# Moving a weight clamp from VectorE to GpSimd, and a subtraction of maxima from ScalarE to VectorE

## The chip, the core and the metric

One core of a Trainium2 chip runs the whole program. Its engines work side by side, each through its own queue in a fixed order: TensorE (PE, with its weight loads listed as PEld), VectorE (DVE), ScalarE (ACT), GpSimd (POOL) and SyncE (SP, which only issues transfers here). The metric is the device time of one execution in microseconds, the median of three runs.

## The reference

A linear attention with random-feature style exponentials feeds a two-layer mixer.

```python
# q, k, v: (8, 8, 576, 64) float32; w_phi: (64, 128) float32
proj = x @ w_phi                                    # for q and for k
proj = proj - max(abs(proj), axis=-1)
phi  = concat([exp(proj), exp(-proj)], axis=-1)     # 256 features
kv, z = k_phi^T @ v, sum_s(k_phi)
attn = (q_phi @ kv) / (q_phi @ z + 1e-6)            # -> x: (8, 576, 512)
u   = x + (relu(x^T @ w_tok1) @ w_tok2)^T           # token mix, 576 -> 256 -> 576
out = u + relu(u @ w_ch1) @ w_ch2                   # channel mix, 512 -> 1536 -> 512
```

The four mixer weights come as float64. The output is float32.

## The kernel before

**Precision.** Most products are made of reduced-width float32 (`F32R`) pieces: each operand is split into a high part and the remainder, and `mm3` (L77) adds three products. The splitting is `split` (L69): one engine casts, another subtracts.

**Five streams.** `keys` (L259) walks over the 32 head pairs: projection `ppk`, the row maximum `mx` of the absolute values (L226), `pm` = projection minus maximum (L228 to L234), two exponentials (L278) and the sums `pkv` (L300). `queries` (L317) does the same for the query side (`ppq`, and `ppt` for the left-over 64 rows), turns `pm` over on TensorE (`pt`, L356), takes exponentials (L363) and forms numerators and denominators (`pn`, L389 and `mm3`), a reciprocal (L401) and the product with it on GpSimd (L402). `token_mix` (L416) runs per batch and per half of the channels, `channel_mix` (L462) per 256 tokens: `h` (up), `acc` (down). `load_weights` (L144) fetches and converts the weights.

**The first four pairs are plain.** For pairs 0 to 3 (`PLAIN = 4`) the attention multiplies whole float32 operands (L216, L389 with 64-row or float32 operands) instead of split ones. `less_max` (L191) tells three cases apart by `base`: `base == D` are the plain keys, `base == 0` the plain queries and their left-over rows, `base is None` the split ones. In the plain cases `pr` is the PSUM bank itself. For plain keys VectorE subtracts the maximum from the bank (L234, `eng` is `nc.vector`). For plain queries VectorE negates the maximum (`nmx`, L230) and ScalarE adds it as a bias, one activation per 128 columns (L232). For the split pairs `pr` is an SBUF tile and GpSimd subtracts (L234).

**The conversion of the weights** is `convert` (L114), called 31 times: 7 times for `w1` and `w2` (tiles named `bits`), 24 times for `wc1` and `wc2` (tiles named `bitsc`, all 128 x 512). A float64 is read as two 32-bit words, `top` and `low`. ScalarE takes the absolute value of `top`, seen as a float32 (L131); VectorE clamps it to `LEAST`, `MOST` (L132), shifts it (L133), puts the sign in (L134) and the highest bits of `low` (L135); ScalarE casts the high part (L72) and GpSimd subtracts it (L75). The tile `m` is one of four buffers with the tag `g`, which `channel_mix` uses too.

**What sets the order.** `weave` (L547) lets the streams take turns by a virtual clock, and so makes the program's order. The scheduler of the language then lays the instructions on each engine's queue, by priority and by a simulated timeline that knows a duration for each instruction. So an edit of one instruction can move its neighbours on every engine. The order is fixed when the program is built; at run time each engine works its queue from front to back and waits on semaphores.

Of the kernel before, what the change touches and what calls it, by code (L numbers as in the profile page):

```python
# [8 lines left out]
F32 = mybir.dt.float32  # L9
# [8 lines left out]
P = 128  # L18
# [24 lines left out]
def mixer_kernel(ctx, tc, qk, vm, vt, w_phi, w1, w2, wc1, wc2d, out):  # L43
# [70 lines left out]
    def convert(hi, lo, srcs, name, tag=None):  # L114

        w, n = hi.shape
        if tag is None:
            tag = f"late{nstage[0] % STAGES}"
            nstage[0] += 1
        raw = wk.tile([P, 4, 256], U32, tag=tag, name=f"raw{name}", bufs=3 if tag == "xt1" else 1)  # L120
        raw = raw.rearrange("p a b -> p (a b)")[:w, :2 * n]
        at = 0
        for src in srcs:
            m = src.shape[1]
            nc.sync.dma_start(raw[:, 2 * at:2 * (at + m)].bitcast(I64), src)
            at += m
        raw = raw.rearrange("p (n two) -> p n two", two=2)
        top, low = raw[:, :, 1], raw[:, :, 0]
        m = streamed(wk, [P, 512], U32, tag="g", name=f"bits{name}", bufs=4)[:w, :n]

        nc.scalar.activation(m.bitcast(F32), top.bitcast(F32), AF.Abs)  # L131
        nc.vector.tensor_scalar(m.bitcast(F32), m.bitcast(F32), LEAST, MOST, op0=ALU.max, op1=ALU.min)  # L132
        nc.vector.tensor_scalar(m, m, 3, 0x3FFFFFF8, op0=ALU.logical_shift_left, op1=ALU.bitwise_and)  # L133
        nc.vector.scalar_tensor_tensor(m, top, 0xC0000000, m, op0=ALU.bitwise_and, op1=ALU.bitwise_or)  # L134
        nc.vector.scalar_tensor_tensor(m, low, 29, m, op0=ALU.logical_shift_right, op1=ALU.bitwise_or)  # L135
        split(hi, lo, m.bitcast(F32), nc.scalar, nc.gpsimd)
# [54 lines left out]
    def less_max(ts, units, name, base=None):  # L191
# [33 lines left out]
        mx = column(wk, 2, tag=f"mx{kind}", name=f"mx{name}")  # L225
        nc.vector.tensor_reduce(mx[:, :n], pr, axis=AX.X, op=ALU.max, apply_absolute_value=True)  # L226
        pm = wk.tile([P, 2, F], F32, tag=f"pm{kind}", name=f"pm{name}", bufs=1 if kind == "t" else 2)
        if base == 0:  # L228
            nmx = column(wk, 2, tag="nmx", name=f"nmx{name}")
            nc.vector.tensor_scalar(nmx[:, :n], mx[:, :n], -1.0, None, op0=ALU.mult)  # L230
            for i in range(n):
                nc.scalar.activation(pm[:, i], pr[:, i], AF.Identity, bias=nmx[:, i:i + 1])  # L232
        else:
            eng.tensor_tensor(pm[:, :n], pr, mx[:, :n].unsqueeze(2).to_broadcast([P, n, F]), op=ALU.subtract)  # L234
        return pm

    nplain = {"k": 0, "q": 0}
# [372 lines left out]
```

## Time and profile before

| | |
|---|---|
| median of three runs | 1180.97 us (1180.92 to 1181.36) |
| profiled execution, span from first to last instruction | 1183.6 us |
| TensorE busy | 1137.6 us (96%) |
| VectorE busy | 867.1 us (73%) |
| ScalarE busy | 531.5 us (45%) |
| GpSimd busy | 587.1 us (50%) |
| mean granted TensorE clock | 0.975 |

The profile holds one execution, a little longer than the runs' median: its span is 2.6 us above it. A time of the page for what lies around the span is not given. Busy shares are averages over the whole span; the program has stretches of different character, so the same numbers by stretch say more. "Idle before" is what an engine stood still ahead of a group, with the engine that released it. The granted clock is the share of TensorE's full speed in a stretch. Where two engines' rows overlap in time at an unusual length, one may be held up by the other without a semaphore.

### The profile page before, as it was taken

The numbers are of one execution on the slowest core, as the hardware profiler recorded it, in microseconds if no ns is written. First come the engines' busy times: TensorE is split into PE (matmuls) and PEld (weight loads), VectorE is DVE, ScalarE is ACT, GpSimd is POOL, SyncE is SP. The second block draws the span as 40 slices with busy tenths as digits, with TensorE's granted clock in tenths as the row PEclk, the third lists the DMA queues.
The fourth block names the chain that finished last, engine by engine and source line by source line (L and its number), as shares of the span: only waits on it lengthen the run. The fifth ranks groups of instructions, "written<-read, shape, count | busy, mean of one in ns | idle before, by whom it ended". The sixth has DMA issues, their size and how long they took to land.

```text
span 1183.6 us, 24087 instructions
## 1 busy us (share of the span) xinstructions
PE 1137.6 (96%) x9032; PEld 1102.0 (93%) x9032; DVE 867.1 (73%) x1782; ACT 531.5 (45%) x1545; POOL 587.1 (50%) x734
## 2 busy tenths in 40 slices
PE   8789897899999999999999999999999999999998
PEld 7667887898999999999999999999999999999998
DVE  7977899986777888887878677684787978763111
ACT  5767565453444445444444443343353544431110
POOL 3344775854555566465555455473564655431000
PEclk9679898999999999999999999999999999999999
DMA  9541222111111111111111011110111110000000
GB/s 232 150 135 28 72 84 71 50 31 28 31 40 32 49 31 32 49 32 49 32 34 46 20 31 49 30 50 1 49 31 49 32 48 12 19 1 19 19 19 19
DMA packets 65300, 54.31 MB, mean 46 GB/s; under 512 B 44768, under 2 KB 56416, under 8 KB 65184
## 3 DMA queue, kind: packets, MB, share of 16 engines
q1 hardware_dynamic: 63824, 52.41, 15.4%
q8 instruction: 72, 1.18, 0.4%
q10 hardware_dynamic: 1360, 0.36, 0.2%
q14 instruction: 44, 0.36, 0.1%
HBM read 43.32 MB, written 9.44 MB: 45 GB/s over the span
## 4 chain that ended last, share of the span: by engine, by line
PE 78%; DVE 11%; ACT 4%; issue 3%; POOL 2%; DMA 2%; SPq 0%; DVEq 0%; POOLq 0%; ACTq 0%
PE h L81 23%; PE acc L81 23%; PE pkv L300 8%; PE pn L81 7%; PE ph L81 3%; PE pa L81 3%; PE pt L356 3%; PE ppq L212 2%; PE ppk L212 2%; DVE qh L74 2%; PE pn L389 1%; DVE den L401 1%; PE px L423 1%; DMA rawc<-in_wc 1%; DVE bitsc L132 1%
## 5 line engine op out<-in xcount | busy, mean ns | idle before, releaser
L81 PE MATMUL acc<-gh,wc 128*128 128x256 f32 x1728 | 345.1, 283 | 0.0
L81 PEld LDWEIGHTS acc<-gh,wc 128*128 128x128 f32 x1728 | 276.0, 188 | 0.2 <-ACT gh L489 0.2
L81 PE MATMUL h<-uh,wc_h 128*128 128x256 f32 x864 | 246.8, 286 | 4.3 <-ACT wc_h L72 2.2
L81 PE MATMUL h<-uh,wc_l 128*128 128x256 f32 x864 | 245.9, 285 | 0.8 <-POOL wc_l L75 0.8
L81 PE MATMUL h<-ul,wc_h 128*128 128x256 f32 x864 | 243.9, 282 | 0.3 <-POOL ul L470 0.3
L81 PE MATMUL acc<-gl,wc 128*128 128x256 f32 x864 | 242.0, 282 | 0.6 <-DVE gl L490 0.6
L278 ACT ACTIVATE kp<-pmk 128x256 f32<-128x256 f32 (+1 forms) x320 | 109.2, 389 | 171.1 <-POOL pmk L234 168.1
L300 PE MATMUL pkv<-v,kp 128*128 128x65 f32 (+1 forms) x1152 | 165.7, 278 | 6.8 <-ACT kp L278 3.3
L81 PEld LDWEIGHTS h<-uh,wc_h 128*128 128x128 f32 x864 | 163.7, 190 | 5.8 <-ACT wc_h L72 2.6
L300 PEld LDWEIGHTS pkv<-v,kp 128*128 128x128 f32 x1152 | 155.9, 200 | 12.6 <-ACT kp L278 5.4
L75 POOL TENSOR_TENSOR ql<-qf,qh 128x320 fp32r<-128x320 f32 (+1 forms) x112 | 103.4, 923 | 127.7 <-DVE qh L74 110.8
L81 PEld LDWEIGHTS h<-uh,wc_l 128*128 128x128 f32 x864 | 163.4, 189 | 1.1 <-POOL wc_l L75 1.1
L81 PEld LDWEIGHTS h<-ul,wc_h 128*128 128x128 f32 x864 | 163.8, 190 | 0.5 <-POOL ul L470 0.5
L81 PEld LDWEIGHTS acc<-gl,wc 128*128 128x128 f32 x864 | 162.5, 188 | 0.7 <-DVE gl L490 0.7
L490 DVE SCALAR_TENSOR_TENSOR gl<-h,gh 128x512 fp32r<-128x512 f32 x108 | 73.5, 680 | 89.2 <-ACT gh L489 88.7
L74 DVE CAST qh<-qf 128x320 fp32r<-128x320 f32 (+1 forms) x224 | 106.5, 489 | 34.6 <-ACT qf L363 29.1
L401 DVE RECIPROCAL den<-den 128x320 f32<-128x320 f32 x64 | 124.6, 1947 | 3.2 <-ACT den L397 2.2
L363 ACT ACTIVATE qf<-pt 128x320 f32<-128x320 f32 (+1 forms) x256 | 92.6, 412 | 71.2 <-PE pt L356 68.5
L81 PE MATMUL pn<-qh,kv 128*128 128x320 f32 (+1 forms) x448 | 118.8, 302 | 3.5 <-DVE qh L74 1.5
L489 ACT ACTIVATE gh<-h 128x512 fp32r<-128x512 f32 x108 | 64.9, 601 | 116.0 <-PE h L81 115.2
L402 POOL TENSOR_TENSOR xt<-xt,den 128x320 f32<-128x320 f32 x64 | 53.7, 839 | 114.7 <-DVE den L401 87.8
L470 POOL TENSOR_TENSOR ul<-xt,uh 128x64 fp32r<-128x64 f32 (+3 forms) x120 | 62.2, 543 | 84.2 <-ACT uh L469 83.3
(110 smaller groups left out, 2415.3 us busy)
## 6 DMA issues: line engine op xcount, KB each, us to landing
raw<-in_qk SPq DMA_DIRECT2D x27, 576.0 KB, 3.7
rawc<-in_wc SPq DMA_DIRECT2D x24, 512.0 KB, 4.2
v<-in_vm SPq DMA_DIRECT2D x31, 256.0 KB, 3.3
out_x<-xt SPq DMA_DIRECT2D x12, 256.0 KB, 2.2
out_x<-xt SPq DMA_DIRECT2D x16, 192.0 KB, 2.0
raw<-in_w SPq DMA_DIRECT2D x8, 256.0 KB, 4.6
out_x<-xt SPq DMA_DIRECT2D x16, 128.0 KB, 1.9
pair<-in_qk SPq DMA_DIRECT2D x8, 160.0 KB, 4.7
```

Source lines behind the costliest of these rows:

```text
L74: eng_hi.tensor_copy(hi, raw)
L75: eng_lo.tensor_tensor(lo, raw, hi.bitcast(F32), op=ALU.subtract)
L81: nc.tensor.matmul(o, a, m, start=first and i == 0, stop=last and i == 2, skip_group_check=group_ok)
L212: nc.tensor.matmul(ps[:, i].rearrange("p two f -> p (two f)"), t[:, c:c + P], wp2.rearrange("p two f -> p (two f)"), start=True, stop=True)
L278: nc.scalar.activation(kp[:, :len(us), sg], pm[:, :len(us)], AF.Exp, scale=1.0 - 2.0 * sg)
L300: nc.tensor.matmul(o, kp[:, n, sg], v, start=g == 0 and n == 0 and sg == 0, stop=u is None, skip_group_check=True)
L363: nc.scalar.activation(full, src, AF.Exp, scale=1.0 - 2.0 * sg)
L401: nc.vector.reciprocal(den, den)
L402: nc.gpsimd.tensor_tensor(x, x, den, op=ALU.mult)
L470: nc.gpsimd.tensor_tensor(l[:, d:d + n], t[:, c, o:o + n], h[:, d:d + n].bitcast(F32), op=ALU.subtract)
L489: nc.scalar.activation(gh, ph, AF.Relu)
L490: nc.vector.scalar_tensor_tensor(gl, ph, 0.0, gh.bitcast(F32), op0=ALU.max, op1=ALU.subtract)
```

## The change

`convert` lets GpSimd do the clamp and swaps its two halves: first the minimum with `MOST`, then the maximum with `LEAST`. `less_max` loses the special case of the plain queries: VectorE now subtracts the broadcast maxima of both 128-column groups from the PSUM bank in one instruction, as for the plain keys. The negation and the activations with a bias go.

```diff
@@ convert @@
         nc.scalar.activation(m.bitcast(F32), top.bitcast(F32), AF.Abs)
-        nc.vector.tensor_scalar(m.bitcast(F32), m.bitcast(F32), LEAST, MOST, op0=ALU.max, op1=ALU.min)
+        nc.gpsimd.tensor_scalar(m.bitcast(F32), m.bitcast(F32), MOST, LEAST, op0=ALU.min, op1=ALU.max)
         nc.vector.tensor_scalar(m, m, 3, 0x3FFFFFF8, op0=ALU.logical_shift_left, op1=ALU.bitwise_and)
@@ less_max @@
         pm = wk.tile([P, 2, F], F32, tag=f"pm{kind}", name=f"pm{name}", bufs=1 if kind == "t" else 2)
-        if base == 0:
-            nmx = column(wk, 2, tag="nmx", name=f"nmx{name}")
-            nc.vector.tensor_scalar(nmx[:, :n], mx[:, :n], -1.0, None, op0=ALU.mult)
-            for i in range(n):
-                nc.scalar.activation(pm[:, i], pr[:, i], AF.Identity, bias=nmx[:, i:i + 1])
-        else:
-            eng.tensor_tensor(pm[:, :n], pr, mx[:, :n].unsqueeze(2).to_broadcast([P, n, F]), op=ALU.subtract)
+        eng.tensor_tensor(pm[:, :n], pr, mx[:, :n].unsqueeze(2).to_broadcast([P, n, F]), op=ALU.subtract)
```

In the changed program the subtraction is L228 (L234 before), and what stands below has numbers lower by six: the reciprocal L395, the product with it L396, `ul` L464. The queues of all engines are laid out anew. What the profile shows behind about 285 us has the same order on every engine in both programs; all that moves stands ahead of that. Three places follow.

VectorE, the second head pair (pair 1), between the subtraction for its fourth key group (`pmk_3`) and the maximum of its fifth (`mxk_4`), which is the next thing that the attention asks of VectorE there. Before:

```order
L234 TENSOR_TENSOR pmk_3_425<-ppk_3_420,mxk_3_423 128x256
L134 SCALAR_TENSOR_TENSOR bitsc_0_0_274<-rawc_0_0_272,bitsc_0_0_274 128x512
L132 TENSOR_SCALAR bitsc_1_0_392<-bitsc_1_0_392 128x512
L135 SCALAR_TENSOR_TENSOR bitsc_0_0_274<-rawc_0_0_272,bitsc_0_0_274 128x512
L133 TENSOR_SCALAR bitsc_1_0_392<-bitsc_1_0_392 128x512
L134 SCALAR_TENSOR_TENSOR bitsc_1_0_392<-rawc_1_0_390,bitsc_1_0_392 128x512
L135 SCALAR_TENSOR_TENSOR bitsc_1_0_392<-rawc_1_0_390,bitsc_1_0_392 128x512
L132 TENSOR_SCALAR bitsc_2_0_557<-bitsc_2_0_557 128x512
L133 TENSOR_SCALAR bitsc_2_0_557<-bitsc_2_0_557 128x512
L134 SCALAR_TENSOR_TENSOR bitsc_2_0_557<-rawc_2_0_555,bitsc_2_0_557 128x512
L132 TENSOR_SCALAR bitsc_3_0_714<-bitsc_3_0_714 128x512
L226 TENSOR_REDUCE mxk_4_468<-ppk_4_466 128x1
```

And in the changed program:

```order
L228 TENSOR_TENSOR pmk_3_411<-ppk_3_406,mxk_3_409 128x256
L135 SCALAR_TENSOR_TENSOR bits_1_246<-raw_1_243,bits_1_246 128x320
L228 TENSOR_TENSOR pmt_431<-ppt_427,mxt_429 128x128
L228 TENSOR_TENSOR pmq_11_398<-ppq_11_393,mxq_11_396 128x256
L133 TENSOR_SCALAR bitsc_0_0_266<-bitsc_0_0_266 128x512
L134 SCALAR_TENSOR_TENSOR bitsc_0_0_266<-rawc_0_0_264,bitsc_0_0_266 128x512
L135 SCALAR_TENSOR_TENSOR bitsc_0_0_266<-rawc_0_0_264,bitsc_0_0_266 128x512
L226 TENSOR_REDUCE mxk_4_449<-ppk_4_447 128x1
```

Ten conversion instructions stood between the two; now four do, and two of the new subtractions. The conversions that are left out here come later, between later steps of the attention. Counted along the queue up to the maximum `mxq_10` of pair 1, which has 21 maxima ahead of it in both programs: 59 conversion instructions ahead of it before (16 of L132, 15 of L133, 15 of L134, 13 of L135), now 28 (10 of L133, 9 and 9). The last instruction of the first 19 conversions has 30 maxima ahead of it in the old queue and 39 in the new one.

GpSimd, where the second block of conversions begins (`bitsc_4` onward), with the split attention running beside it. Before:

```order
L402 TENSOR_TENSOR xt_1_1326<-xt_1_1326,den_1_1535 128x256
L75 TENSOR_TENSOR ql_001_1811<-qf_001_1808,qh_001_1810 128x320
L234 TENSOR_TENSOR pmq_01_1837<-pq_01_1833,mxq_01_1835 128x256
L234 TENSOR_TENSOR pmk_2_1914<-pk_2_1910,mxk_2_1912 128x256
L187 TENSOR_TENSOR stq_2242<-raw_2217,stq_2242 64x512
L75 TENSOR_TENSOR wc_4_1704<-bitsc_4_1707,wc_4_1704 128x512
L234 TENSOR_TENSOR pmq_10_1982<-pq_10_1978,mxq_10_1980 128x256
```

And in the changed program:

```order
L396 TENSOR_TENSOR xt_1_1270<-xt_1_1270,den_1_1479 128x256
L75 TENSOR_TENSOR wc_4_1648<-bitsc_4_1651,wc_4_1648 128x512
L132 TENSOR_SCALAR bitsc_5_1710<-bitsc_5_1710 128x512
L228 TENSOR_TENSOR pmq_01_1781<-pq_01_1777,mxq_01_1779 128x256
L132 TENSOR_SCALAR bitsc_6_1786<-bitsc_6_1786 128x512
L75 TENSOR_TENSOR ql_001_1755<-qf_001_1752,qh_001_1754 128x320
L228 TENSOR_TENSOR pmk_2_1858<-pk_2_1854,mxk_2_1856 128x256
L187 TENSOR_TENSOR stq_2186<-raw_2161,stq_2186 64x512
L75 TENSOR_TENSOR wc_5_1707<-bitsc_5_1710,wc_5_1707 128x512
L228 TENSOR_TENSOR pmq_10_1926<-pq_10_1922,mxq_10_1924 128x256
```

The clamps, each of which waits for ScalarE's absolute value, stand in one queue with the attention's subtractions `pmq`, `pmk`, `ql` and `stq`; `ql_001` of the same pair now has two clamps and the remainder `wc_4` ahead of it. The last product of the conversion (`wc_5`) has moved up by several rows of attention.

ScalarE, the first query group of pair 0. Before:

```order
L131 ACTIVATE bits_0_132<-raw_0_129 128x512
L232 ACTIVATE pmt_125<-ppt_121,nmxt_126 128x128
L232 ACTIVATE pmq_00_145<-ppq_00_140,nmxq_00_146 128x128 x2
L278 ACTIVATE kp_2_223<-pmk_2_221 128x2x128 x2
L131 ACTIVATE bits_3_176<-raw_3_173 128x512
```

And in the changed program:

```order
L131 ACTIVATE bits_0_130<-raw_0_127 128x512
L131 ACTIVATE bits_3_171<-raw_3_168 128x512
L131 ACTIVATE bits_2_188<-raw_2_186 64x256
L272 ACTIVATE kp_2_215<-pmk_2_213 128x2x128 x2
L131 ACTIVATE bits_0_200<-raw_0_198 128x256
```

The activations with a bias are gone, and the absolute values for the next weight tiles move up.

## The prediction

> **What bounds the kernel now.** I began with the page's slices, to see where TensorE is not full, then cut the span into stretches, then asked in those for groups by shape and for waits. The slices: engine, then the busy tenths of 40 slices of 29.6 us each, and the granted clock.
>
> ```profile
> span 1183.6 us, 24087 instructions
> PE   8789897899999999999999999999999999999998
> DVE  7977899986777888887878677684787978763111
> PEclk9679898999999999999999999999999999999999
> ```
>
> After the eighth slice TensorE is full at full clock; ahead of it both are broken. The busy time by stretch says more (length, then busy time and count of PE, PEld, DVE, ACT, POOL, then the clock):
>
> ```profile
> 25.00:75.00 50.00, 42.19 (x179) 32.32 (x179) 48.20 (x93) 35.94 (x96) 19.05 (x15) 0.69 0.56 165
> 75.00:110.00 35.00, 31.82 (x178) 25.18 (x176) 22.76 (x41) 24.82 (x75) 13.91 (x13) 0.86 0.19 58
> 110.00:150.00 40.00, 36.36 (x250) 33.44 (x250) 34.31 (x74) 24.40 (x73) 27.61 (x34) 0.91 0.20 59
> 150.00:225.00 75.00, 63.21 (x463) 59.84 (x462) 74.28 (x124) 41.01 (x106) 51.06 (x52) 0.93 0.22 65
> 225.00:300.00 75.00, 73.13 (x602) 71.37 (x601) 54.77 (x117) 35.05 (x105) 41.56 (x53) 1.00 0.16 46
> 300.00:1000.00 700.00, 691.25 (x5774) 683.74 (x5773) 541.94 (x1149) 311.73 (x940) 389.53 (x494) 1.00 0.12 35
> ```
>
> From 225 us on TensorE does 602 matmuls in 75 us and idles 1.9 us; nothing that the edit touches can be bought there, and the order there is the old one. In 150 to 225 us VectorE is busy 74.28 of 75 us, TensorE idles 11.8 us and does 463 matmuls. In 25 to 75 us VectorE is busy 48.20 of 50, TensorE idles 7.8 us, and the clock granted to what it does is 0.69. So two stretches are bound by VectorE, and both hold the conversions: the clamps' own busy time there is
>
> ```profile
> 25.00:75.00 50.00, 9.54 (x13) 0.69 0.56 165
> 150.00:225.00 75.00, 8.05 (x12) 0.93 0.22 65
> ```
>
> and none of it lies between 75 and 150 us. Whatever shortens these two stretches shortens the end, since the rest follows in a fixed order behind them.
>
> **What VectorE's time there is made of.** Groups by shape in 25 to 75 us, then the same four of the conversion in 150 to 225 us, then the first weight tiles of the same shape (`bits`), which met little else:
>
> ```profile
> L134 DVE SCALAR_TENSOR_TENSOR bitsc<-rawc,bitsc 128x512 uint32<-128x512 uint32 x12 | 10.9, 916 | 0.1
> L132 DVE TENSOR_SCALAR bitsc<-bitsc 128x512 f32<-128x512 f32 x12 | 9.2, 769 | 0.1
> L135 DVE SCALAR_TENSOR_TENSOR bitsc<-rawc,bitsc 128x512 uint32<-128x512 uint32 x12 | 9.0, 759 | 0.0
> L133 DVE TENSOR_SCALAR bitsc<-bitsc 128x512 uint32<-128x512 uint32 x12 | 5.6, 473 | 0.0
> L234 DVE TENSOR_TENSOR pmk<-ppk,mxk 128x256 f32<-128x256 f32 x8 | 3.2, 404 | 0.0
> L230 DVE TENSOR_SCALAR nmxq<-mxq 128x2 f32<-128x2 f32 x6 | 0.9, 156 | 0.0
> ...
> L134 DVE SCALAR_TENSOR_TENSOR bitsc<-rawc,bitsc 128x512 uint32<-128x512 uint32 x12 | 12.6, 1052 | 0.1
> L135 DVE SCALAR_TENSOR_TENSOR bitsc<-rawc,bitsc 128x512 uint32<-128x512 uint32 x12 | 9.9, 835 | 0.1
> L132 DVE TENSOR_SCALAR bitsc<-bitsc 128x512 f32<-128x512 f32 x12 | 8.1, 678 | 0.0
> L133 DVE TENSOR_SCALAR bitsc<-bitsc 128x512 uint32<-128x512 uint32 x12 | 7.9, 658 | 0.1
> ...
> L134 DVE SCALAR_TENSOR_TENSOR bits<-raw,bits 128x512 uint32<-128x512 uint32 x2 | 1.4, 686 | 0.0
> L135 DVE SCALAR_TENSOR_TENSOR bits<-raw,bits 128x512 uint32<-128x512 uint32 x2 | 1.4, 676 | 0.0
> L132 DVE TENSOR_SCALAR bits<-bits 128x512 f32<-128x512 f32 x2 | 0.8, 424 | 0.3 <-ACT bits L131 0.3
> L133 DVE TENSOR_SCALAR bits<-bits 128x512 uint32<-128x512 uint32 x2 | 0.8, 422 | 0.0
> ```
>
> A free conversion costs VectorE 686 + 676 + 424 + 422 = 2208 ns. In the first stretch it costs 916 + 769 + 759 + 473 = 2917, in the second 1052 + 835 + 678 + 658 = 3223. The difference is GpSimd's doing, as one place of the timeline shows:
>
> ```profile
> 33.95 1.47 POOL L75 TENSOR_TENSOR wc_l<-bitsc,wc_h 128x512 fp32r<-128x512 f32 x1 [3.91 <-ACT wc_h L72]
> 34.32 1.65 DVE L134 SCALAR_TENSOR_TENSOR bitsc<-rawc,bitsc 128x512 uint32<-128x512 uint32 x1
> 35.63 1.49 POOL L75 TENSOR_TENSOR wc_l<-bitsc,wc_h 128x512 fp32r<-128x512 f32 x1 [0.21 <-ACT wc_h L72]
> 35.89 1.51 DVE L132 TENSOR_SCALAR bitsc<-bitsc 128x512 f32<-128x512 f32 x1
> ```
>
> An instruction of 0.69 or 0.42 us on VectorE that starts inside one of GpSimd ends only after it. I call this a lock. It takes 12 x 709 ns = 8.5 us of the first stretch, 0.45 us for each us that GpSimd is busy (19.05), and 12 x 1015 ns = 12.2 us of the second, 0.24 us for each (51.06). The Trainium skill (SBUF — State Buffer, section Who interferes with whom) describes it: one pair of ports, taken for a whole instruction by a VectorE operation with two SBUF inputs or in a two-port mode, or by GpSimd. The rows agree. A subtraction that reads PSUM (L234, 404 ns) shows no such length.
>
> **The change, part by part.** *The price of the clamp on GpSimd* has no row. GpSimd's nearest ones, over the whole run:
>
> ```profile
> L75 POOL TENSOR_TENSOR wc<-bitsc,wc 128x512 fp32r<-128x512 f32 x12 | 15.7, 1309 | 14.1 <-ACT wc L72 14.0
> L470 POOL TENSOR_TENSOR ul<-xt,uh 128x128 fp32r<-128x128 f32 x32 | 14.1, 467 | 0.3
> L470 POOL TENSOR_TENSOR ul<-xt,uh 128x64 fp32r<-128x64 f32 x32 | 11.7, 370 | 19.7 <-ACT uh L469 19.5
> masks.py:199 POOL TENSOR_SCALAR_AFFINE_SELECT ident<-ident 128x128 f32<-128x128 f32 x1 | 0.3, 292 | 0.0
> ```
>
> With two inputs 512 columns take 1309 ns; this is the upper bound, 1.31 us. From 128 to 512 columns that is (1309 - 467) / 384 = 2.2 ns a column, hence about 190 ns fixed. The one row with a single input, 128 columns in 292 ns, leaves 100 ns for them, 0.8 ns a column: 0.19 + 512 x 0.8 ns = 0.6 us. With a fixed part of 230 ns it would be 0.48 us, the lower bound. I take 0.7 us: near the row with a single input, with something for the second operation. The Trainium skill (GPSIMD Engine Reference, section Engine selection) calls one-input work roughly line-rate; with 512 columns at 1.2 GHz, an estimate of 0.43 us beside the fixed part, the sum below would gain about 1 us more.
>
> *First stretch, VectorE's load.* Out: 13 clamps, 9.54 us. Of it 13 x 0.424 = 5.5 are work at most, and 4.0 lock. The lock falls on what comes next as well; I let half of it stay: -7.5 (between -9.5 and -5.5). In: lock by 13 clamps on GpSimd, 13 x 0.7 x 0.45 = +4.1 (0.48 us: +2.8; 1.31 us: +7.7). The stretch's eight negations go, 8 x 156 ns = 1.2 us, and eight subtractions come, 8 x 404 ns = 3.2: +2.0. Sum -1.4, between -4.7 and +4.2. By load alone the first stretch stays as it is. GpSimd has room: 19.05 of 50 us, and 9.1 more.
>
> *First stretch, order.* This is the larger term. The pairs' maxima and subtractions get ahead of conversions: up to `mxq_10` of pair 1 the new queue has 15 shifts and sign and bit steps fewer ahead of it, beside the 16 clamps. At (916 + 759 + 473) / 3 = 716 ns that is 10.7 us that the attention need not wait for. The conversions so put off are for matrices that nothing reads before the first `h`, and VectorE has room for them, 12.2 us idle in 75 to 110 and 5.7 in 110 to 150:
>
> ```profile
> 113.72 1.76 DVE den L401
> 151.70 2.89 PE h L81 x24
> ...
> 219.60 1.49 DVE bitsc L135
> ```
>
> These are from the chain of waits: the last reciprocal of pair 3, behind which the first batch can be mixed, the first up-projection, and the last step of the last conversion. What the attention can gain by it is bounded by TensorE's idle time up to there, 7.8 + 3.2 = 11.0 us in 25 to 110, since its matmuls are the same; with a higher clock it could be more. The chain also runs along TensorE's own matmuls in part, so I take under half: -5 for the stretch, load included (0 to -11). ScalarE's part, 36 activations less, I cost at nothing by itself: it is busy 35.94 of 50 us there, and two instructions in a row become one earlier on VectorE.
>
> ```profile
> L232 ACT ACTIVATE pmq<-ppq,nmxq 128x128 f32<-128x128 f32 x32 | 10.1, 366 | 4.7 <-DVE nmxt L230 3.0 <-DVE nmxq L230 1.5
> ```
>
> Were that cover gone, these 10.1 us would be the most it gives. Between 110 and 150 us no engine is full and the gain is handed on.
>
> *Second stretch.* No plain pair is left, so only the clamps count. Out: 8.05 us, of which 12 x 0.424 = 5.1 work and 3.0 lock; half of the lock stays: -6.5. In: 12 x 0.7 x 0.24 = +2.0 lock (1.31 us: +3.8). Net -4.5, between -6.7 and -1.3. Against it stands the queue: a conversion now goes ScalarE, GpSimd, VectorE instead of ScalarE, VectorE, and clamps stand ahead of `ql`, `pmq` and `pmk`, for which the attention waits; GpSimd goes from 51.06 to about 61.5 busy of 75 us. I charge +2.0 for that. Net -2.5.
>
> Sum: -5 - 2.5 = -7.5 us, all ahead of 285 us. The profiled span of 1183.6 would become 1176; the runs' median lies 2.6 us under the span, so 1180.97 becomes **1173.5 us**.
>
> **The rivals.**
>
> *Larger.* If VectorE no longer starves TensorE in the first stretch, the clock comes back too: at 0.69 the 42.19 us busy hold 29 us of full-speed time. Half of that 13 us on top gives 1173.5 - 6.5 = 1167. For it: the clock is low just where VectorE is full, and 1.00 from 225 us on. Against: it would need an attention that TensorE alone paces.
>
> *No change.* VectorE and GpSimd take turns at the lock, so work moved from one to the other stays in the same line; the order gains nothing, because TensorE's own chain paces the pairs, and the longer way through three engines eats the second stretch. -1.4 at most: 1180. For it: the load sum of the first stretch. Against: 4.0 and 3.0 us of the clamps' own lock are gone. The Trainium skill (Perfetto Trace Analysis, section Optimizing Scalar/DVE Operations) says that offloading between these two might not help.
>
> *Slower.* The clamp costs GpSimd what a subtraction costs, 1.31 us, and its queue becomes the bound in 150 to 225 us. 51.06 + 12 x 1.31 = 66.8 us busy; and of its 24 us idle before, part is waiting for VectorE's casts and maxima that no order removes:
>
> ```profile
> POOL ql L75 <- DVE qh L74: 6.1, 3, 2.4
> POOL pmq L234 <- DVE mxq L226: 3.9, 2, 2.0
> ```
>
> With these 10 us it stands at 77 of 75, and every subtraction comes late: +2 there, and the first stretch's upper bound of +4.2 us: 1187. It decides from about 1.1 us a clamp.
>
> **How the numbers follow.** Chances: the forecast 0.50, larger 0.15, no change 0.20, slower 0.15. The range reaches from below the larger case (1163) to just short of the slower one, 1185; the forecast's own is 1169 to 1178. A change under 0.2% (2.4 us) can't be told from none. Faster takes the forecast but for a twentieth, and the larger case: 0.63; within 0.2%: 0.21; slower: 0.16.
>
> **What would show it.** Right, if in the new profile VectorE's conversions of the first block reach past 75 us while the last reciprocal of pair 3 comes before 110 us, the granted clock in 25 to 75 us lies above 0.69, a clamp takes 0.5 to 0.9 us on GpSimd, and the first `h` starts 3 to 8 us earlier; the last `bitsc` step then ends earlier than at 221 us. The subtractions of the plain queries should take 0.4 us with none over 0.5. Wrong, if the clamp takes over 1.1 us, if GpSimd has no idle time left in the second stretch, or if the rows behind 285 us, in their old order, gain or lose by themselves more than 2 us.

## The result, and the profile after

The changed kernel takes 1188.99 us in the median (1185.95 to 1190.31), the kernel before 1180.95 beside it: a ratio of 1.0058, with a 95% interval of 1.0038 to 1.0077. A second set of executions of both gave 1186.62 against 1182.65 us and a ratio of 1.0027 (1.0013 to 1.0041). The change costs 3 to 7 us; I had forecast a gain of 7.5.

The head of the page of the changed kernel, as the prediction showed it of the one before (span; then PE, DVE and the granted clock in 40 slices of 29.6 us):

```profile
span 1184.2 us, 24079 instructions
PE   8988878799999999999999999999999999999998
DVE  6997997866778878877878577684687978763111
PEclk9969988899999999999999999999999999999999
```

TensorE's second slice is better than before, in busy time (9 for 7) and in clock (9 for 6); the third has the lower clock (6 for 7). From the third to the eighth its tenths sum up to 46 instead of 49.

Single executions of the kernel before lie between 1179 and 1189 us, and the profile in the prediction is of one from the upper part; so I compare a second pair of profiles, whose executions lie at the medians. Windows of the second profile of the kernel before (length; busy time and count of PE, PEld, DVE, ACT, POOL; clock):

```profile
25.00:75.00 50.00, 41.64 (x183) 32.33 (x183) 47.78 (x95) 35.94 (x95) 19.33 (x16) 0.73 0.57 167
75.00:110.00 35.00, 31.87 (x202) 25.29 (x203) 25.57 (x48) 29.08 (x87) 15.02 (x14) 1.00 0.22 70
150.00:225.00 75.00, 63.32 (x462) 59.79 (x461) 72.65 (x122) 40.08 (x104) 53.42 (x53) 0.93 0.22 66
```

and of the changed kernel:

```profile
25.00:75.00 50.00, 45.92 (x255) 37.43 (x253) 48.75 (x89) 37.95 (x98) 30.75 (x32) 0.90 0.56 170
75.00:110.00 35.00, 28.51 (x159) 23.24 (x159) 28.03 (x47) 22.91 (x63) 18.77 (x18) 0.85 0.28 87
150.00:225.00 75.00, 57.73 (x398) 53.24 (x396) 65.07 (x109) 39.21 (x105) 59.06 (x63) 0.90 0.22 66
```

In 25 to 75 us TensorE does 255 matmuls instead of 183, at a clock of 0.90 instead of 0.73. In 150 to 225 us it does 398 instead of 462, though VectorE is busy for 7.6 us less there (65.07 for 72.65). Both engines wait: VectorE for 9.9 us of the 75 and TensorE for 17.3, where the kernel before has 2.4 and 11.7. How far each kernel is at the end of the first block tells the last reciprocal of pair 3; how far at the end of the second, the last step of the last conversion. From VectorE's timeline (start, duration, instruction), the kernel before:

```profile
110.31 1.75 DVE L401 RECIPROCAL den<-den 128x256 f32<-128x256 f32 x1 [0.35 <-ACT den L397]
...
215.63 1.69 DVE L135 SCALAR_TENSOR_TENSOR bitsc<-rawc,bitsc 128x512 uint32<-128x512 uint32 x1
```

and the changed kernel:

```profile
104.85 1.75 DVE L395 RECIPROCAL den<-den 128x256 f32<-128x256 f32 x1 [0.61 <-ACT den L391]
...
229.46 0.84 DVE L135 SCALAR_TENSOR_TENSOR bitsc<-rawc,bitsc 128x512 uint32<-128x512 uint32 x1
```

The changed kernel is 5.5 us ahead at 105 us and 13.0 us behind at 230. From 293 us on, where the order is the same again, it stays 4 to 5 us behind; the spans differ by 4.9 (1185.2 and 1180.3). So the second stretch lost 10.4 us. The clock has little part in that: by the prediction's way of reckoning, an estimate, a clock of 0.90 in 150 to 225 us takes 57.73 x 0.10 = 5.8 us of TensorE's busy time, and the 0.93 of before 63.32 x 0.07 = 4.4. That loss is what the experiments are about.

### The profile page after: what moved, and what is told of

Read it like the earlier page. It is cut to its first block, busy times and chain, and to the rows that moved or that the text cites. A ratio compares the mean times of both kernels' runs of the same rounds, so it can differ in the third digit from the quotient of the medians.

```text
span 1184.2 us, 24079 instructions
## 1 busy us (share of the span) xinstructions
PE 1134.9 (96%) x9032; PEld 1100.6 (93%) x9032; DVE 858.0 (72%) x1751; ACT 522.5 (44%) x1509; POOL 607.6 (51%) x765
## 4 chain that ended last, share of the span: by engine, by line
PE 75%; DVE 12%; issue 4%; ACT 4%; POOL 3%; DMA 1%; DVEq 0%; POOLq 0%; SPq 0%; ACTq 0%
PE h L81 23%; PE acc L81 23%; PE pkv L294 8%; PE pn L81 6%; PE ph L81 3%; PE pa L81 3%; PE pt L350 2%; DVE qh L74 2%; PE ppk L212 2%; PE ppq L212 2%; DVE ql L75 1%; PE px L417 1%; DVE bitsc L134 1%; DVE den L395 1%; DVE mxk L226 1%
## 5 line engine op out<-in xcount | busy, mean ns | idle before, releaser
L81 PE MATMUL acc<-gh,wc 128*128 128x256 f32 x1728 | 349.8, 286 | 1.7 <-ACT gh L483 0.8
L484 DVE SCALAR_TENSOR_TENSOR gl<-h,gh 128x512 fp32r<-128x512 f32 x108 | 73.4, 680 | 90.7 <-ACT gh L483 90.2
L395 DVE RECIPROCAL den<-den 128x320 f32<-128x320 f32 x64 | 124.7, 1948 | 4.2 <-ACT den L391 3.1
L396 POOL TENSOR_TENSOR xt<-xt,den 128x320 f32<-128x320 f32 x64 | 54.8, 856 | 115.3 <-DVE den L395 81.2
L464 POOL TENSOR_TENSOR ul<-xt,uh 128x64 fp32r<-128x64 f32 (+3 forms) x120 | 62.0, 541 | 80.4 <-ACT uh L463 79.5
```

What stands on the lines that cost most here:

```text
L81: nc.tensor.matmul(o, a, m, start=first and i == 0, stop=last and i == 2, skip_group_check=group_ok)
L395: nc.vector.reciprocal(den, den)
L396: nc.gpsimd.tensor_tensor(x, x, den, op=ALU.mult)
L464: nc.gpsimd.tensor_tensor(l[:, d:d + n], t[:, c, o:o + n], h[:, d:d + n].bitcast(F32), op=ALU.subtract)
L484: nc.vector.scalar_tensor_tensor(gl, ph, 0.0, gh.bitcast(F32), op0=ALU.max, op1=ALU.subtract)
```

## The experiments

All were timed beside the kernel before, whose median was 1182.0 to 1182.7 us each time. The ratio is formed from the runs, not from the two medians; 0.1% is 1.2 us. Differences between two kernels below are differences of their ratios. The edits are shown shortened.

| kernel | median us | ratio (95%) |
|---|---|---|
| before, again | 1182.03 | 0.9992 (0.9972 to 1.0011) |
| changed, again | 1186.62 | 1.0027 (1.0013 to 1.0041) |
| subtraction alone | 1186.26 | 1.0020 (1.0000 to 1.0040) |
| clamps alone | 1186.08 | 1.0034 (1.0009 to 1.0059) |
| first 19 clamps on GpSimd | 1181.30 | 0.9991 (0.9976 to 1.0006) |
| last 12 clamps on GpSimd | 1192.95 | 1.0065 (1.0042 to 1.0089) |
| first 19, last 12 without clamp | 1171.94 | 0.9908 (0.9882 to 0.9933) |
| the same, with 12 idle clamps | 1177.86 | 0.9949 (0.9929 to 0.9968) |
| last 12 remainders on VectorE | 1181.93 | 0.9994 (0.9978 to 1.0010) |
| first 25 clamps on GpSimd | 1180.91 | 0.9975 (0.9958 to 0.9991) |
| first 29 clamps on GpSimd | 1188.92 | 1.0051 (1.0031 to 1.0071) |
| `ul` of one group on VectorE | 1185.58 | 1.0025 (1.0013 to 1.0038) |
| eight buffers, changed | 1183.00 | 1.0005 (0.9982 to 1.0027) |
| eight buffers, before | 1187.93 | 1.0036 (1.0014 to 1.0057) |
| first 19, casts on ScalarE | 1175.68 | 0.9948 (0.9923 to 0.9972) |
| the same, again | 1175.48 | 0.9926 (0.9905 to 0.9947) |
| first 25, casts on ScalarE | 1184.45 | 1.0016 (0.9999 to 1.0032) |
| before, casts on ScalarE | 1180.03 | 0.9982 (0.9962 to 1.0002) |

The first theory was a queue: in the second block the clamps stand in GpSimd's in-order queue behind the attention's and the channel mix's subtractions, and the lead is lost there.

### Which part, and which block

Four kernels each take one part of the change. Subtraction and first 19 clamps (conversions counted from 1 to 31, the second block has 20 to 31):

```diff
-        nc.gpsimd.tensor_scalar(m, m, MOST, LEAST, op0=ALU.min, op1=ALU.max)
+        (nc.gpsimd if nconv <= 19 else nc.vector).tensor_scalar(...)
```

> The changed kernel with the clamps of the first 19 conversions on GpSimd and those of the last 12 back on VectorE. Queue theory (in the second block the clamps stand in GpSimd's in-order queue behind the channel mix's and the attention's subtractions, and that alone costs): the first block keeps its gain of about 10 us at the last reciprocal of pair 3 (103 instead of 113.7 us), the second block goes as before the change, the time is about 1171 us (1167 to 1175). Rival, give-back (whatever the first block gains, the second is paced by something that starts at its own time, so that the lead is lost in any case): 1178 to 1183. Rival, subtraction (what costs is the subtraction of the plain queries on VectorE): 1185 or more.

Subtraction and last 12 clamps (`nconv > 19`):

> The changed kernel with the clamps of the last 12 conversions on GpSimd and those of the first 19 back on VectorE. Queue theory: little is gained ahead of 110 us, and the second block loses what it loses in the changed kernel, some 10 us: 1188 to 1196 us. Give-back: about the time of the changed kernel, 1186 to 1190, since the second block alone sets it. Subtraction: 1180 to 1185 in the second block's favour, with the loss ahead of 110 us.

The clamps alone, the biased activations kept:

> All clamps on GpSimd; the plain queries keep the negation on VectorE and the biased activations on ScalarE. Queue theory: the time of the changed kernel, 1186 to 1191 us, since the subtraction has no part in the second block. Subtraction theory: faster than the kernel before, 1170 to 1177.

The subtraction alone, the clamps kept on VectorE:

> The subtraction of the plain queries on VectorE; all clamps stay there too. Queue theory: within 2 us of the kernel before, 1179 to 1183 us: VectorE pays about 2 us of load in the first stretch, ScalarE is freed of 10 us that were mostly hidden. Subtraction theory: 1185 to 1190.

None of the theories had all four. The first 19 clamps on GpSimd bring 0.29% beside the subtraction (0.9991 against 1.0020; against the last-12 kernel 0.38%), 3.4 to 4.5 us. The last 12 cost 0.36% (1.0027 against 0.9991) or 0.45% (1.0065 against 1.0020), 4.3 to 5.3 us. So the clamps of the second block lose what those of the first gain, and more. The subtraction can't be told from nothing: alone it costs 0.20%, with an interval that begins at 1.0000, and beside all clamps it brings 0.07% (1.0027 against 1.0034). The queue theory was wrong on the 19: it wanted 1171 us, the gain of the first block kept. VectorE's timeline of the kernel with 19:

```profile
103.61 1.75 DVE L400 RECIPROCAL den<-den 128x256 f32<-128x256 f32 x1 [0.61 <-ACT den L396]
```

It is 6.7 us ahead of the kernel before at that place, and its span of 1179.4 us is 0.9 shorter. Most of the lead is given back even with the second block's clamps on VectorE: the give-back rival had that right, with its 1178 to 1183. The subtraction theory has the median of the subtraction alone (1186.26), but it wanted 1170 to 1177 us for the clamps alone, which take 1186.08. In the profile of the subtraction alone the same reciprocal is 3.3 us ahead of before,

```profile
106.97 1.75 DVE L395 RECIPROCAL den<-den 128x256 f32<-128x256 f32 x1 [0.46 <-ACT den L391]
```

but with the last 12 clamps on GpSimd beside it, and the first 19 on VectorE, it starts at 110.81 us, 0.5 us behind. Two profiles of the kernel before differ by 3.4 us at that place. How much of the first stretch's lead the subtraction brings is therefore not shown. The one profile of the clamps alone is of an execution 9 us above that kernel's median, and I draw nothing from its times.

### What the spread and the second pair of profiles say

> The kernel before, unchanged: a second profile of it and the spread of its executions. The first profile lies 2.6 us above the median then measured. If the low granted clock of 0.69 in 25 to 75 us belongs to slow executions of the kernel before, this profile (if it lies near 1181 us) has a clock nearer to 0.8 there and the last reciprocal of pair 3 ends 3 to 6 us ahead of 115.5 us; then the gain of the changed kernel's first block is that much smaller than the first pair of profiles shows. If the spread comes later, the last reciprocal of pair 3 stays at 115 us.

> The changed kernel, unchanged, beside the others of this call: a second profile and the spread. Queue theory: between 187 and 191 us in the median, the clamps of the second block again behind a run of GpSimd's subtractions, with VectorE idle for over 5 us in 150 to 225 us.

The first guess was half right: the clock in 25 to 75 us is hardly better in the second profile of the kernel before (0.73 for 0.69), but in 75 to 110 us it is 1.00 for 0.86, and the last reciprocal of pair 3 ends 3.4 us earlier. The gain of the first stretch is 5.5 us between typical executions, not the 10.7 that the first pair of profiles shows. The changed kernel again takes longer, with a median just under the range expected (the recorded 187 stands for 1187 us), and with VectorE idle for 9.9 of 75 us (65.07 busy) where the kernel before has 2.4.

### What VectorE's time in the second block is worth

```diff
-        nc.gpsimd.tensor_scalar(m, m, MOST, LEAST, op0=ALU.min, op1=ALU.max)
+        if nconv <= 19: nc.gpsimd.tensor_scalar(...)
```

> The first 19 clamps on GpSimd, the last 12 left out altogether (this kernel leaves out the clamp of the weights' bits in the second block). It bounds what taking the clamp from VectorE in the second block can bring. If VectorE's time paces that block, the 5 us of work and 3 us of lock that go make it 4 to 8 us faster than with those clamps on VectorE: 1173 to 1177 us. If GpSimd's and TensorE's own chains pace it (the give-back), within 2 us of it: 1179 to 1183.

It is 0.83% faster than the kernel with those clamps on VectorE, 9.8 us, for twelve clamps that are busy for 10.4 us in that kernel's profile. So the reading that VectorE bounds the second block is right: about the whole busy time of the clamps, with what GpSimd adds to it, is on the path. And 1.19%, 14.1 us, lie between this kernel and the changed one, which differ by 12 clamps on GpSimd. The next kernel lets GpSimd do such a clamp for nothing:

```diff
+        else:
+            nc.gpsimd.tensor_scalar(idle, top, MOST, LEAST, op0=ALU.min, op1=ALU.max)
```

> As the kernel without the last 12 clamps, but GpSimd does an idle clamp of the same size for each of them, from the weight's top words into a tile that nothing reads (the weights' own bits of the second block stay without a clamp). GpSimd has the changed kernel's load in the second block, and no conversion waits for it. Path theory (the long way of a conversion over three engines is what costs the 14.7 us between 1171.9 and 1186.6): 1171 to 1176 us. Load theory (GpSimd's time, with the lock and with later subtractions for the attention, costs it): 1181 to 1187.

0.9949 lies between the two theories: 4.8 us of the 14.1 are there. It isn't as clean as meant, because an idle clamp waits for the weights' transfer alone; five of the twelve ran ahead of 150 us, and GpSimd is busy for 52.0 us in 150 to 225 and not 59. Its order is laid out anew as well. So it speaks for a cost of the load alone, and it does not say that the other 9.3 us are all the longer way.

### GpSimd's load, or the place in a queue

The remainders of the last 12 conversions go to VectorE:

```diff
-        split(hi, lo, m.bitcast(F32), nc.scalar, nc.gpsimd)
+        split(hi, lo, m.bitcast(F32), nc.scalar, nc.gpsimd if nconv <= 19 else nc.vector)
```

> All clamps on GpSimd as in the changed kernel; of the last 12 conversions VectorE computes the remainder that GpSimd computed (1.3 us each there, the nearest row on VectorE is about 0.7 us). GpSimd loses 15.7 us of the second block and VectorE gets 8.4 us. Queue theory (the clamps come late because GpSimd's queue is full): the loss goes for the larger part, 1179 to 1184 us, and no clamp is waited for longer than 1.5 us. Route theory (a conversion that passes from ScalarE to GpSimd to VectorE is late by the handing over itself, and VectorE's load counts): 1188 to 1194.

It gave back 0.33%, 3.9 us, as the queue theory wanted, although VectorE has 72.62 busy of 75 us again. Then the number of clamps on GpSimd was varied, 25 and 29:

> The changed kernel with the clamps of the first 25 conversions on GpSimd, those of the last 6 on VectorE. In the changed kernel the first six conversions of the second block ended 7 to 10 us earlier than in the kernel before, the last ones 9 to 13 us later. If the loss comes from the place in the queue (behind the channel mix's subtractions, from 180 us on), these six clamps are a gain: 1174 to 1179 us, under the 1181.3 of the kernel with 19. If each clamp on GpSimd in the second block costs alike, it lies between 1181 and 1187: 1183 to 1185.

> The changed kernel with only the last two clamps (bitsc_10 and bitsc_11, the two that stand in GpSimd's queue behind the eight subtractions ul of the channel mix) back on VectorE; the rest of GpSimd's queue is the old one. If the loss comes from the place of these two, it goes for the larger part: 1179 to 1182 us, about the kernel with 25. If it comes evenly from the last six or twelve clamps, a third of what 25 clamps gave back: 1184 to 1186.

With 25 the loss is gone (0.9975), with 29 all of it is there (1.0051). Neither time was expected: with 25 it lies between the two cases, with 29 above both. Taking the last two clamps back, the ones that I had seen behind `ul`, brings nothing; the step lies between 25 and 29 clamps, 0.76% or 9 us. That killed the theory of the place behind `ul`. Next, `ul` itself was taken out of GpSimd's fullest stretch, all clamps on GpSimd and the other order as it was:

```diff
-                nc.gpsimd.tensor_tensor(l[:, d:d + n], ...)
+                (nc.vector if i == 1 else nc.gpsimd).tensor_tensor(l[:, d:d + n], ...)
```

> The changed kernel, all 31 clamps on GpSimd, with one thing else: the eight subtractions ul of the channel mix's second group of 256 tokens (5.4 us of GpSimd at 210 to 216 us, just where its queue has no gap) on VectorE, which stands idle for 3 us there; the rest of GpSimd's order is the same. If a full GpSimd in 199 to 228 us is what TensorE waits for (ql of pair 5 after 3.5 us, the weights' remainders after it): TensorE's wait for ql is under 0.5 us, the last conversion ends 4 to 6 us earlier than at 230 us, and the time falls by 4 to 6 us, to 1181 to 1183. If the loss sits elsewhere in the second block (the wait at 175 to 190 us): 1185 to 1188.

TensorE's longest wait in 205 to 225 us (in all, times, longest), in the changed kernel and then in this one:

```profile
PE pn L81 <- POOL ql L75: 3.5, 1, 3.5
...
PE pn L81 <- DVE qh L74: 3.6, 1, 3.6
```

The wait for `ql` went, and one of the same length for VectorE's `qh` came in its place: the eight `ul`, at 214.0 to 217.5 us, now stand ahead of `qh` on VectorE. The last conversion ended at 231.7 us, no earlier, and the time did not move: 1.0025. One wait was traded for another, so this run doesn't settle whether a full GpSimd there is the cause. The expectation's other branch names another place, 175 to 190 us, and I looked there next.

### What happens at 184 us

VectorE's timeline in the changed kernel:

```profile
183.14 0.41 DVE L75 TENSOR_TENSOR xl<-px,xh 128x256 fp32r<-128x256 f32 x1
183.47 0.40 DVE L226 TENSOR_REDUCE mxk<-pk 128x2 f32<-128x256 f32 x1
187.84 0.76 DVE L307 TENSOR_TENSOR kv<-pkv,kv 128x256 fp32r<-128x256 f32 x2 [3.97 <-ACT kv L305]
188.51 0.42 DVE L133 TENSOR_SCALAR bitsc<-bitsc 128x512 uint32<-128x512 uint32 x1
188.85 1.75 DVE L395 RECIPROCAL den<-den 128x256 f32<-128x256 f32 x1
```

GpSimd's at the same time:

```profile
184.78 1.19 POOL L132 TENSOR_SCALAR bitsc<-bitsc 128x512 f32<-128x512 f32 x2
190.68 1.27 POOL L396 TENSOR_TENSOR xt<-xt,den 128x256 f32<-128x256 f32 x1 [4.71 <-DVE den L395]
```

The clamps of conversions 26 and 27 are done at 186.0 us, on a GpSimd that then has nothing to do. Their shifts could run on VectorE, which has nothing to do either. But in its queue they stand behind `kv`, and `kv` waits 3.97 us for ScalarE's cast, which waits for TensorE. VectorE in the kernel with 25 clamps on GpSimd, whose instructions on VectorE, ScalarE and GpSimd are the same up to there (1 us later in this execution):

```profile
184.44 0.40 DVE L231 TENSOR_REDUCE mxk<-pk 128x2 f32<-128x256 f32 x1
184.77 0.73 DVE L137 TENSOR_SCALAR bitsc<-bitsc 128x512 f32<-128x512 f32 x1
185.53 0.72 DVE L138 TENSOR_SCALAR bitsc<-bitsc 128x512 uint32<-128x512 uint32 x1
186.28 0.70 DVE L139 SCALAR_TENSOR_TENSOR bitsc<-rawc,bitsc 128x512 uint32<-128x512 uint32 x1
187.01 0.69 DVE L140 SCALAR_TENSOR_TENSOR bitsc<-rawc,bitsc 128x512 uint32<-128x512 uint32 x1
187.62 0.42 DVE L137 TENSOR_SCALAR bitsc<-bitsc 128x512 f32<-128x512 f32 x1
188.08 0.43 DVE L138 TENSOR_SCALAR bitsc<-bitsc 128x512 uint32<-128x512 uint32 x1
189.69 0.76 DVE L312 TENSOR_TENSOR kv<-pkv,kv 128x256 fp32r<-128x256 f32 x2 [1.19 <-ACT kv L310]
```

The same wait is there, and it is filled: with both clamps on VectorE, six steps of the two conversions stand ahead of `kv`, 3.7 us of work in what is a hole in the changed kernel. The scheduler lays the steps out by its own simulated times; with the clamp on GpSimd it puts what follows the clamp behind `kv`, and the real `kv` is late. With 29 clamps the wait is 4.7 us. In 175 to 190 us (windows, one kernel each; the third engine is DVE) the changed kernel has

```profile
175.00:190.00 15.00, 10.17 (x64) 9.31 (x63) 10.75 (x19) 7.89 (x20) 7.96 (x10) 0.77 0.18 57
```

the one with 29,

```profile
175.00:190.00 15.00, 10.74 (x52) 9.61 (x53) 10.03 (x18) 7.37 (x19) 8.79 (x10) 0.56 0.21 68
```

the one with `ul` on VectorE,

```profile
175.00:190.00 15.00, 9.99 (x43) 8.52 (x42) 10.64 (x20) 6.60 (x16) 9.80 (x11) 0.56 0.25 73
```

the one with 25,

```profile
175.00:190.00 15.00, 10.18 (x45) 9.06 (x46) 13.37 (x24) 7.24 (x18) 7.96 (x8) 0.54 0.28 88
```

and the one with the remainders on VectorE:

```profile
175.00:190.00 15.00, 11.86 (x77) 10.79 (x76) 14.64 (x30) 8.00 (x21) 8.13 (x10) 0.77 0.20 67
```

VectorE is busy for 10.75, 10.03 and 10.64 us of 15 in the three that take longer, and for 13.37 and 14.64 in the two that don't. So in these five the hole goes with the loss.

It is not where TensorE loses, though. TensorE's work ahead of the hole, around and behind it, and close to the end of the second block, in the kernel before (second profile),

```profile
175.00:183.00 8.00, 5.93 (x48) 5.41 (x46) 8.00 (x17) 4.92 (x12) 4.02 (x6) 1.00 0.34 114
183.00:215.00 32.00, 25.38 (x179) 24.29 (x179) 31.44 (x51) 17.12 (x42) 20.18 (x22) 0.89 0.12 39
215.00:225.00 10.00, 9.44 (x76) 9.15 (x77) 8.37 (x15) 3.45 (x11) 9.38 (x9) 1.00 0.16 32
```

in the changed kernel,

```profile
175.00:183.00 8.00, 3.17 (x16) 2.31 (x14) 7.72 (x13) 3.52 (x10) 4.99 (x7) 0.75 0.33 106
183.00:215.00 32.00, 29.21 (x204) 27.45 (x205) 26.63 (x50) 18.33 (x50) 23.55 (x25) 0.90 0.14 43
215.00:225.00 10.00, 5.52 (x30) 5.11 (x28) 5.92 (x10) 4.49 (x12) 9.83 (x12) 0.75 0.18 59
```

and with 25 clamps on GpSimd:

```profile
175.00:183.00 8.00, 4.01 (x16) 2.97 (x16) 7.69 (x13) 3.41 (x10) 5.33 (x5) 0.57 0.38 127
183.00:215.00 32.00, 28.08 (x183) 27.19 (x183) 28.78 (x51) 18.45 (x47) 18.40 (x19) 0.79 0.12 34
215.00:225.00 10.00, 9.50 (x79) 9.24 (x79) 9.42 (x15) 3.77 (x11) 9.77 (x11) 1.00 0.07 16
```

Two losses can be told apart. The first is the lead of the first block. In 175 to 183 us, ahead of the hole, TensorE does 16 matmuls instead of 48, in the changed kernel and with 25 clamps alike. It waits there for VectorE's `qh` (2.5 and 2.4 us; with 19 clamps 3.6) and `xl` (1.5 and 1.1 us). By the channel mix's `gl` (L484, L490 before) the changed kernel is 8.1 us ahead at the third and only 0.7 us at the fourth.

The second loss parts the changed kernel from the one with 25 clamps. In the 32 us that hold the hole the changed kernel does more matmuls than the other two, 204. In 215 to 225 us it does 30, where the others do 76 and 79; with 29 clamps it is 30 as well. There TensorE waits 3.5 us for the `ql` shown above (3.1 with 29 clamps, and not at all with 25). VectorE had finished its part of it at 213.9 us; GpSimd, which has no gap from 206.6 to 225.0 us, begins it at 218.6. VectorE stands still for a clamp in the same queue:

```profile
218.68 0.94 DVE L133 TENSOR_SCALAR bitsc<-bitsc 128x512 uint32<-128x512 uint32 x1 [3.05 <-POOL bitsc L132]
```

That is GpSimd's queue, as the first theory had it, some 30 us behind the hole. The kernel before has such a wait too, 2.3 us for `pmq`, just ahead of 215 us. Whether the steps that were put off behind `kv` are what fills GpSimd later is open. One kernel speaks against it: with 25 clamps and the casts on ScalarE (below) there is no hole at 184 us (VectorE is busy for 14.84 of 15), and TensorE does only 30 matmuls in 215 to 225 us all the same. Two kernels with the last 12 clamps on GpSimd, the one without the first 19 and the one without the subtraction, have no such hole either, and take longer.

VectorE's idle time in 150 to 225 us is no measure of the loss. It is 9.9 us in the changed kernel, 8.8 with 29 clamps, 4.3 with 25 and 2.4 in the kernel before, but 7.9 and 6.4 us in the two profiles of the fastest whole kernel, with the casts on ScalarE. A kernel that changes nothing but the place of the shifts behind `kv`, or of `ql` in GpSimd's queue, wasn't tried. So it is shown that clamps 26 to 29 on GpSimd cost the 9 us, and that TensorE falls behind mostly in 215 to 225 us; which of the waits is the cause is not shown.

### Buffers

`m` shares four buffers with `gh` and `gl`, and holds one longer on the way over three engines. In both kernels the three `bufs=4` became 8.

> The changed kernel with eight buffers of the tag g instead of four (m of the conversions, gh and gl of the channel mix). In the profiles a conversion of the second block holds its buffer, from the absolute value to the remainder, for 13.7 us in the mean of twelve in the changed kernel and for 11.2 in the kernel before. Buffer theory (the longer way over three engines holds the four buffers, so that fewer conversions and gh, gl are under way): the loss goes, 1176 to 1182 us, and the last conversion ends ahead of 222 us. Order theory (what is late is late in the engines' fixed order, buffers or not): 1184 to 1189, the last conversion after 226 us.

> The kernel before with eight buffers of the tag g, as a control. Buffer theory: it gains less than the changed kernel does, since its conversions hold a buffer for 11.2 us: 1178 to 1182. If four buffers are a limit in any case, both gain alike. Order theory: within 2 us of 1182.

The changed kernel improved by 0.22% (2.6 us); the control took 0.36% longer, above all that was expected of it. The changed one's last conversion ends at 226.0 us, between the two expectations. That one gains where the other loses speaks for the buffers, but both programs are laid out anew by it, and the first difference is no larger than its interval. The buffers stay open as a part of the cause.

### A version that is faster than both

VectorE bounds the second block, ScalarE is busy for half of it. The casts of the stacked heads `stk` and `stq` (L186) of head pairs 4 to 8 ("heads" in the expectations) go to ScalarE:

```diff
-            nc.vector.tensor_copy(t[base:base + D], src)
+            (nc.scalar.copy if int(name[1:]) <= 8 else nc.vector.tensor_copy)(t[base:base + D], src)
```

With 19 clamps on GpSimd, and a second time:

> The kernel with 19 clamps on GpSimd, and in it the casts of the stacked heads (stk and stq, VectorE, about 0.7 us each, some 7 of them in 150 to 225 us) of heads 4 to 8 on ScalarE, which is busy for only 37 of 75 us there. If VectorE's time paces the second block, as the kernel without the last 12 clamps says (-9.4 us for 8.05 us of clamps), these 5 us give 3 to 6: 1175 to 1178 us. If ScalarE's place in the chain takes it back: 1180 to 1184.

> The kernel with 19 clamps on GpSimd and the stacked heads' casts of heads 4 to 8 on ScalarE a second time, since its executions spread over 12 us: if it is faster than the kernel before, the median is again under 1179 us and the ratio's interval under 1; if the first result was a lucky set, 1179 to 1182.

With 25 clamps, and on the kernel before:

> The kernel with the stacked heads' casts of heads 4 to 8 on ScalarE, with 25 clamps on GpSimd instead of 19. With 19 it took 1175.7 us. If six clamps more or less in the middle of the second block are worth nothing (1180.9 with 25, 1181.3 with 19): 1174 to 1177.

> The kernel before with the stacked heads' casts of heads 4 to 8 on ScalarE, all clamps on VectorE and the biased activations as they were. If VectorE's time in the second block is what counts, this alone gives about what it gave beside the 19 clamps (-5.6 us): 1176 to 1179 us. If it needs the lead that the first block's clamps on GpSimd give, 1180 to 1183.

With 19 clamps it held twice: 0.9948 and 0.9926, about 1175.5 us, 6 to 9 us faster than the kernel before. In 150 to 225 us, its second profile:

```profile
150.00:225.00 75.00, 61.56 (x446) 58.87 (x445) 68.64 (x114) 43.21 (x109) 49.85 (x51) 0.91 0.22 67
```

VectorE has 4 us less than in the kernel before and ScalarE 3 us more. The other two gave no such gain. On the kernel before the casts bring 0.18%, not told from nothing; with 25 clamps, where I expected 1174 to 1177, the time is 1184.45. An order that is laid out anew moves the time by several us in either direction, and a sum of engine times doesn't see that.

## Why the prediction was wrong

**What bounds the kernel** was read rightly: the second block's clamps, taken off VectorE and put nowhere, are worth 9.8 us.

**The price of the clamp** was right: 0.70 us taken, and over the run (groups by shape, the changed kernel)

```profile
L132 POOL TENSOR_SCALAR bitsc<-bitsc 128x512 f32<-128x512 f32 x24 | 18.6, 778 | 9.5 <-ACT bitsc L131 9.3
```

778 ns in the mean, the shortest 607. The Trainium skill (GPSIMD Engine Reference, section Engine selection) calls one-input work roughly line-rate; the prediction's estimate from it, 0.43 us, and its fixed part of 0.19 us make 0.62 us, close to the shortest. The two clamps at 184.78 us, with VectorE idle beside them, took 1.19 us together. So the mean seems to hold what GpSimd loses to VectorE. The plain subtractions took 411 ns and none over 0.43, as said.

**First stretch**, -5 us with the load: the last reciprocal of pair 3 came 5.5 us earlier, conversions of the first block reached to 91 us, the clock in 25 to 75 us rose to 0.90 (in 75 to 110 us it fell from 1.00 to 0.85), and the first `h` started 4.4 us earlier, at 109.6 for 114.0 us, inside the 3 to 8. The row at 151.70 us that I had quoted as the first up-projection is the first on the chain; `h` begins at 117.4 us in that profile. "Between 110 and 150 us no engine is full and the gain is handed on" was true up to 150 us. Behind it the lead is lost: in 175 to 183 us TensorE waits 4.0 us for VectorE's `qh` and `xl`, and its clock is 0.75 where it was 1.00. With the second block's clamps back on VectorE the ratio is 0.9991, so 1.1 us of the 5 arrive.

**Second stretch** is the step that failed: "Net -2.5", made of -6.5 for VectorE's load, +2.0 for the lock and +2.0 for the queue. VectorE's busy time did fall, by 7.6 us, but the last 12 clamps on GpSimd cost 4.3 us at the end instead of bringing 2.5. The clamps off VectorE are worth 9.8 us, and putting them on GpSimd costs 14.1, where the sum had 4.0 for lock and queue. The prediction's place was right in kind: an attention's `ql` is late in GpSimd's queue, 3.5 us at 219 us for that one wait alone, and a conversion waits 3.05 us for its clamp beside it. What it left out is VectorE's queue, where the steps that follow a clamp can end up behind a `kv` that waits 3.97 us; the order rows that I had quoted show GpSimd's side only. How the 14.1 us divide between these is open. A slip besides: 51.06 + 12 x 0.7 makes 59.5 us of GpSimd's busy time and not 61.5; 59.06 was measured.

**The rivals.** "Slower" has nearly the right time, 1187, in part by luck: a clamp costs 0.78 and not 1.31 us, the first stretch did not lose, and GpSimd keeps 15.9 us idle in the second; but a late subtraction for the attention is there. "No change" said that work moved between the two engines stays in the same line, and that the longer way through three engines eats the second stretch. For the whole change that comes nearest, though the lock is not the reason: the three steps left on VectorE took 1082, 765 and 761 ns in the second stretch, in sum as long as before (1054, 682 and 834). Its sentence from the Trainium skill (Perfetto Trace Analysis, section Optimizing Scalar/DVE Operations), that offloading between the two might not help, agrees with 1.0027 for the whole change and 1.0034 for the clamps alone; the first 19 clamps, which bring 0.29%, are an exception to it. "Larger" did not come.

**The sign that I named for the tail** was right: behind 290 us the two kernels run alike to within 1 us in the second pair of profiles. The one for the second block was not: the last `bitsc` step, which should have ended ahead of 221 us, ended at 230.

## What to carry to other kernels

A step that moves from the bounding engine to another stands in a new queue, and so does what follows it. Look in the new queues of both engines for the next wait on a slow producer (here `kv` on VectorE), for what the bottleneck waits for (here `ql` on GpSimd), and count which ready work stood ahead of it before and stands behind it now. Then check the suspicion on the engine that must be full: TensorE's matmuls, counted by stretch beside a kernel that doesn't lose, put the loss some 30 us behind the most conspicuous hole. And judge a gain of 0.5% in a kernel whose order is laid out anew by more than one profile of each: of two profiles of one kernel here, the first was 3.4 us later than the second at the same step.

## What was not expected of the hardware

The granted clock differs between executions of one program, over nearly the same work: in 75 to 110 us of the second profile of the kernel before it is 1.00, and in 78.4 to 113.4 us of the first, whose steps come 3.4 us later there, 0.90. And twelve clamps taken from VectorE, where it is full, gave 9.8 us. They were busy for 10.4 us there, while at the 424 ns of a free one they would be 5.1 us of work. The intervals of the two ratios leave about 3.5 us either way, so the length that GpSimd's neighbourhood adds to VectorE's instructions seems to count like work; no run separates it.
